# Batch 0 of a spectral layer multiplied in whole float32, and part of batch 1's first DFT placed ahead of the first feed-forward chunk

## The chip, the cores and the metric

The kernel runs on one core of one Trainium2 chip. The metric is the time of one execution in microseconds (us), lower is better. A core has a matmul engine (PE, with its weight loads shown as PEld), a vector engine (DVE), an activation engine (ACT), a general engine (POOL) and a queue (SP) that in this kernel issues all the DMAs. The engines run beside each other, each strictly in the order of its own instructions, and wait for each other through semaphores.

## The reference

```python
X = np.fft.rfft(x, axis=1)                      # x: 8 batches, 3008 times, 256 features
Yr = Xr @ w_r - Xi @ w_i + b_r                  # complex 256x256 linear layer
Yi = Xr @ w_i + Xi @ w_r + b_i
Yr = np.sign(Yr) * np.maximum(np.abs(Yr) - 0.01, 0.0)     # soft threshold, Yi likewise
y = np.fft.irfft(Yr + 1j * Yi, n=3008, axis=1)
h = y.reshape(24064, 256) @ w_in                # w_in, w_out: float64, 2048 wide
out = (h - np.tanh(h)) @ w_out
```

## The kernel before

The transform of length 3008 = 64 x 47 is done in two steps each way, all as matmuls. For each batch:

- **forward** (class `Forward`): 8 loads of `xt` (96 x 4 x 256), each in two parts of 512 columns. A part is multiplied by the constant `f1` (94 x 96) and written as `a` to a scratch tensor in DRAM.
- **spectrum** (class `Spectrum`): 12 units `jp`. Each reads back one `at` tile (128 x 512) of `a`, does the second DFT step with four matmuls (line 277), the linear layer (`cross` and `shared`, line 299), the threshold (`shrink`, line 334 onward), and the first inverse step with the constant `i1` (`inverse`, lines 359 to 361), and writes `z` to DRAM.
- **FFN** (class `Chunk`): 470 columns of time at a time. `time` reads five column groups of `z` as `zin` and does the second inverse step (line 394), `up` multiplies by `w_in` (line 407) and takes h - tanh(h), `down` multiplies by `w_out` (line 428). There are 16 steps `f` to a chunk; chunks 0 and 1 run interleaved as the first 32 steps.

Most products are made with a **split**: an operand is cast on ACT to a float32r part `hi` (line 90), DVE or POOL subtracts it to give `lo` (line 91), and three float32r matmuls (`hi·lo`, `lo·hi`, `hi·hi`) replace one float32 matmul. Two products run in whole float32 already: line 277 and line 394. A whole float32 matmul appears in the trace as two PE records, a float32r one as one.

The float64 weights come as raw words (`w_raw`, 512 KB a piece, 16 pieces) and are rebuilt on the chip. I call that a conversion here: six DVE instructions, three on ACT and two on POOL for each piece (`split_f64`, lines 164 to 180).

The order up to the first FFN step is written out by hand: warm-up matmuls, the whole forward stage of batch 0, the 12 spectrum units of batch 0 with four conversions spread between them, three more conversions, then `time` of chunks 0 and 1. In the loop over `i`, unit `i` is transformed while unit `i-1` is multiplied, unit `i-2` is thresholded and an older one goes through `inverse`. After that a table of slots (`put`, `run`) hangs the remaining conversions, the forward stage of batch 1 (16 parts from slot 8 on) and later batches onto the FFN steps; there the order on each engine is set by a scheduler.

Tiles come from pools with a few buffers for each tag; a tile that takes a buffer waits until its last reader is done. DMAs are issued by SP in program order, so one that waits for a buffer holds back all that are queued behind it.

Of the kernel before, what the change touches and what calls it, by code (L numbers as in the profile page):

```python
# [66 lines left out]
def spectral_ffn(ctx, tc, x, w_r, w_i, b_r, b_i, w_in, w_out, f1, f2, i1, i2, out):  # L67
# [31 lines left out]
    def split_const(ap, shape, name, queue):  # L99
        t = work.tile(shape, F32, name=f"{name}_f", tag="tmp", bufs=4)  # L100
        queue.dma_start(out=t, in_=ap)
        return split(t, name)

    def load_linear():
        wr = load.tile([P, 2, D], F32, name="wr_f", tag="at", bufs=3)
# [8 lines left out]
    def split_linear(wr, wi, bias, zero):  # L114
        w2 = work.tile([P, 2, D], F32, name="w2_f", tag="tmp", bufs=4)
        w3 = work.tile([P, 2, D], F32, name="w3_f", tag="tmp", bufs=4)
# [11 lines left out]
        w3 = split(w3, "w3")  # L128
        w2 = split(w2, "w2", rest=nc.gpsimd)
        w1 = split(wr, "w1", rest=nc.gpsimd)  # L130
        return w1, w2, w3, bias, (ones, brow)
# [67 lines left out]
    class Forward:  # L199
# [15 lines left out]

        def dft(self, q):
# [32 lines left out]
    class Spectrum:  # L249
        def __init__(self, b, jp, first=False):  # L250
            self.b, self.jp, self.first = b, jp, first
            self.rest = nc.gpsimd if first and jp < NJ // 2 - 2 else nc.vector

        def temp(self, name, tag):
            if self.first:
                return ffn.tile([P, 2, D], F32, name=name, tag=tag)
            return work.tile([P, 2, D], F32, name=name, tag="tmp", bufs=4)
# [7 lines left out]
        def dft(self):  # L265
            self.dft0()
            self.dft1()
            self.sums()

        def dft0(self):  # L270
            ps = self.ps = ps_f.tile([P, 512], F32, name="ps_f2", tag="f")
            pv = ps.rearrange("p (t r j m) -> p t j r m", t=2, r=2, j=2)
            for jj in range(2):
                o = m0[2 * self.jp + jj]
                rhs = f2t.rearrange("p (r u c) -> p r u c", r=2, u=2)[:, :, :, o:o + 32]
                for t in range(2):
                    nc.tensor.matmul(pv[:, t, jj], self.at[:, jj, t * P:(t + 1) * P], rhs, start=True, stop=True)  # L277
            self.xh = work.tile([P, 2, 2, P], F32R, name="xh", tag="sp_h", bufs=3)
# [3 lines left out]
            xi = self.xi = work.tile([P, 2, P], F32, name="xi")  # L282
            nc.scalar.copy(out=xi, in_=ps.rearrange("p (t r m) -> p t r m", t=2, r=2)[:, :, 1, :])

        def dft1(self):
            ps, xi = self.ps, self.xi
            flat = "p t r m -> p (t r m)"
            nc.vector.tensor_tensor(out=self.xl.rearrange(flat), in0=ps, in1=self.xh.bitcast(F32).rearrange(flat), op=ALU.subtract)
            pr = ps.rearrange("p (t r m) -> p t r m", t=2, r=2)
            nc.vector.tensor_tensor(out=xi, in0=pr[:, :, 0, :], in1=xi, op=ALU.add)  # L290

        def sums(self):
            self.s = split(self.xi, f"s_{self.b}_{self.jp}", work, "s")

        def product(self, dst, hi, lo, w, more=False, last=True):
            n = 0
            for lhs, rhs in ((lo, w[0]), (hi, w[1]), (hi, w[0])):
                for t in range(2):
                    nc.tensor.matmul(dst, lhs[:, t], rhs[:, t, :], start=n == 0 and not more, stop=n == 5 and last)  # L299
                    n += 1  # L300

        def cross(self, k):
            if k == 0:
                if self.first:
                    self.vv = ps_h.tile([P, 512], F32, name="ps_v", tag="h")
                    ones, brow = lin[4]
                    nc.tensor.matmul(self.vv, ones, brow, start=True, stop=False)
                else:
                    self.vv = ps_f.tile([P, 512], F32, name="ps_v", tag="f")
                self.product(self.vv[:, :D], self.xh[:, :, 1], self.xl[:, :, 1], lin[2], self.first, not self.first)  # L310
            else:
                self.product(self.vv[:, D:], self.xh[:, :, 0], self.xl[:, :, 0], lin[1], self.first)

        def shared(self):
            if self.first:
                t1 = ps_o.tile([P, 512], F32, name="ps_t1", tag=f"o{self.jp % 2}")
            else:
                t1 = ps_f.tile([P, 512], F32, name="ps_t1", tag="f")
            self.product(t1[:, :D], *self.s, lin[0])
            tb = self.tb = self.temp("tb", "th")  # L320
            if self.first:
                nc.scalar.copy(out=tb[:, 0, :], in_=t1[:, :D])
            else:
                nc.vector.tensor_tensor(out=tb, in0=t1[:, :D].unsqueeze(1).to_broadcast([P, 2, D]), in1=lin[3], op=ALU.add)
            if not self.first:
                self.shrink()
                self.halves()

        def shrink(self):
            tb = self.tb  # L330
            y = self.temp("y", "g")
            for jj in range(2):
                for ri in range(2):
                    nc.vector.tensor_tensor(  # L334
                        out=y[ri * 64:(ri + 1) * 64, jj, :],
                        in0=tb[jj * 64:(jj + 1) * 64, 0 if self.first else ri, :],
                        in1=self.vv[jj * 64:(jj + 1) * 64, ri * D:(ri + 1) * D],
                        op=ALU.add,
                    )
            mn = work.tile([P, 2, D], F32, name="mn", tag="tmp", bufs=4)  # L340
            if self.first and self.rest is nc.gpsimd:
                up = self.temp("up", "th")
                nc.scalar.activation(out=up, in_=y, func=AF.Relu, bias=below)
                nc.vector.tensor_scalar(out=mn, in0=y, scalar1=LAM, scalar2=0.0, op0=ALU.add, op1=ALU.min)
                self.rest.tensor_tensor(out=mn, in0=up, in1=mn, op=ALU.add)
            else:
                nc.vector.tensor_scalar_min(out=mn, in0=y, scalar1=-LAM)
                nc.vector.scalar_tensor_tensor(out=mn, in0=y, scalar=LAM, in1=mn, op0=ALU.max, op1=ALU.add)
            self.mn = mn

        def halves(self):
            where = (ffn, "g", None) if self.first else (work, "sp", 3)
            self.z = split(self.mn, f"z_{self.b}_{self.jp}", *where, rest=self.rest)

        def inverse(self):
# [5 lines left out]
            nc.tensor.matmul(pzv, i1h, zh, start=False, stop=True)  # L361
            zo = work.tile([P, 512], F32, name="zo", tag="tmp", bufs=4)
            nc.scalar.copy(out=zo, in_=pz)
            nc.sync.dma_start(out=rows(z_dram[self.b], self.jp), in_=zo)

# [80 lines left out]
    def plan_forward(b, start, each, ahead):  # L446
        for ch in range(NP // XC):
# [5 lines left out]
    def plan_spectrum(b, start, each, ahead, lag, first=False):  # L453
        for jp in range(NJ // 2):
            s = Spectrum(b, jp, first)
# [19 lines left out]
    with tc.manual_schedule(engines={E.PE, E.Activation, E.DVE, E.Pool, E.SP}):  # L475
# [5 lines left out]
        for i in range(11):  # L481
# [3 lines left out]
        f1h, f1l = split_const(f1, [94, 96], "f1", nc.sync)  # L485
        first = [Forward(0, ch) for ch in range(NP // XC)]
        for f in first[:4]:
            f.load()
        lin_in = load_linear()
        f2t = load_const(f2, [P, 384], "f2")  # L490
# [122 lines left out]
```

## Time and profile before

| | us |
|---|---|
| median of 3 runs | 2736.25 (2736.23 to 2739.11) |
| profiled execution, its own time | 2735.33 |
| its span, first to last instruction | 2733.2 |
| PE busy | 2680.9 (98%) |
| DVE busy | 1772.7 (65%) |
| ACT busy | 1393.0 (51%) |
| POOL busy | 80.0 (3%) |

Rows of a timeline give start, duration, engine, line, operation, output<-input, shape, count, and in brackets the idle time before it with what ended that. Rows of a table of stretches give the length, then busy time and count for each engine, the granted PE clock (1.00 is full), the busy share of the DMA engines and GB/s. PE ends are modelled and overlap the next start, so I take the distance of starts where I can.

### The profile page before, as it was taken

What the parts mean: (1) busy time and instruction counts of PE and PEld (TensorE: products, weight loads), DVE (VectorE), ACT (ScalarE), POOL (GpSimd) and SP (SyncE); (2) the same over time, 40 slices, a digit from 0 to 9 for tenths busy, and PEclk for the clock granted to TensorE, in tenths of its full rate; (3) what the DMA queues carried; (4) which work ended last, traced back from release to release, by engine and by line L of the source; (5) the groups of instructions that cost most, each with busy time, mean ns of one, the idle gap of its engine ahead of it and who ended that gap; (6) DMA issues with size and microseconds to landing.
All of it is one profiled execution on the core that took longest, in us unless ns stands there. A gap on an engine that the chain in (4) does not pass through costs nothing.

```text
span 2733.2 us, 37167 instructions
## 1 busy us (share of the span) xinstructions
PE 2680.9 (98%) x14199; PEld 2392.5 (88%) x14199; DVE 1772.7 (65%) x3084; ACT 1393.0 (51%) x2628; POOL 80.0 (3%) x59
## 2 busy tenths in 40 slices
PE   7699999999999999999999999999999999999999
PEld 5578888999989998899988999889998999998989
DVE  6996776666656766576755666656665666655555
ACT  4565455445464545554455444644546444444445
POOL 2540000000000000000000000000000000000000
PEclk7899999999999999999999999999999999999999
DMA  6442114111131112311114111321104111100000
GB/s 191 124 119 85 50 49 126 49 38 44 37 114 47 43 38 74 89 42 49 35 43 116 42 38 38 101 66 45 53 22 123 41 46 40 35 22 22 19 19 17
DMA packets 105026, 163.50 MB, mean 60 GB/s; under 512 B 7472, under 2 KB 70960, under 8 KB 104752
## 3 DMA queue, kind: packets, MB, share of 16 engines
q1 hardware_dynamic: 104848, 161.13, 19.5%
q8 instruction: 112, 1.84, 0.3%
q14 instruction: 66, 0.54, 0.1%
HBM read 86.13 MB, written 74.97 MB: 59 GB/s over the span
## 4 chain that ended last, share of the span: by engine, by line
PE 91%; DVE 4%; ACT 1%; issue 1%; DMA 0%; POOL 0%; SPq 0%; DVEq 0%; ACTq 0%; POOLq 0%
PE o L428 36%; PE h L407 36%; PE ps_v L299 5%; PE ps_i L394 4%; PE ps_f L277 3%; PE ps_t L299 2%; PE ps_f L220 1%; PE ps_f L222 1%; DVE y L334 1%; PE ps_f L221 1%; PE ps_i L360 1%; PE ps_i L361 1%; PE ps_i L359 1%; DVE g L412 1%; DVE gl L416 0%
## 5 line engine op out<-in xcount | busy, mean ns | idle before, releaser
L412 DVE TENSOR_TENSOR g<-h,th 128x470 f32<-128x470 f32 (+1 forms) x832 | 531.7, 639 | 559.0 <-ACT th L410 551.3
L410 ACT ACTIVATE th<-h 128x470 f32<-128x470 f32 (+1 forms) x832 | 463.1, 557 | 771.0 <-PE h L407 769.3
L416 DVE TENSOR_TENSOR gl<-g,gh 128x470 fp32r<-128x470 f32 (+1 forms) x832 | 531.5, 639 | 289.3 <-ACT gh L414 205.5
L414 ACT CAST gh<-g 128x470 fp32r<-128x470 f32 (+1 forms) x832 | 483.0, 581 | 389.4 <-DVE g L412 381.1
L428 PE MATMUL o<-gh,wout_l 128*128 128x470 f32 (+1 forms) x1664 | 632.5, 380 | 0.1
L428 PE MATMUL o<-gl,wout_h 128*128 128x470 f32 (+1 forms) x1664 | 616.6, 371 | 2.2 <-DVE gl L416 2.2
L428 PE MATMUL o<-gh,wout_h 128*128 128x470 f32 (+1 forms) x1664 | 615.8, 370 | 0.0
L407 PE MATMUL h<-yh,win_l 128*128 128x470 f32 (+1 forms) x1664 | 481.9, 370 | 3.0 <-DVE g L412 2.9
L407 PE MATMUL h<-yl,win_h 128*128 128x470 f32 (+1 forms) x1664 | 480.8, 370 | 0.0
L407 PE MATMUL h<-yh,win_h 128*128 128x470 f32 (+1 forms) x1664 | 480.6, 370 | 0.0
L428 PEld LDWEIGHTS o<-gl,wout_h 128*128 128x128 f32 x1664 | 312.8, 188 | 43.9 <-DVE gl L416 5.2
L407 PEld LDWEIGHTS h<-yh,win_l 128*128 128x128 f32 x1664 | 310.4, 188 | 41.8 <-DVE g L412 6.3
L428 PEld LDWEIGHTS o<-gh,wout_l 128*128 128x128 f32 x1664 | 313.1, 188 | 35.3 <-DVE ot L437 1.3
L407 PEld LDWEIGHTS h<-yl,win_h 128*128 128x128 f32 x1664 | 310.9, 188 | 35.7
L407 PEld LDWEIGHTS h<-yh,win_h 128*128 128x128 f32 x1664 | 311.0, 188 | 35.6
L428 PEld LDWEIGHTS o<-gh,wout_h 128*128 128x128 f32 x1664 | 313.6, 188 | 32.2
L334 DVE TENSOR_TENSOR y<-tb,ps_v 64x256 f32<-64x256 f32 x384 | 160.0, 417 | 3.9
L394 PEld LDWEIGHTS ps_i<-i,zin 96*128 96x128 f32 x1024 | 130.2, 197 | 13.3 <-issue 10.4
L394 PE MATMUL ps_i<-i,zin 96*128 96x94 f32 x1024 | 131.9, 278 | 9.7 <-DMA zin<-z 9.7
L91 DVE TENSOR_TENSOR x_l<-xt,x_h 94x512 fp32r<-94x512 f32 x128 | 91.6, 724 | 48.3 <-ACT x_h L90 48.2
L277 PE MATMUL ps_f<-f,at 128*128 128x128 f32 x768 | 104.3, 278 | 11.9 <-DMA at<-a 11.9
L277 PEld LDWEIGHTS ps_f<-f,at 128*128 128x128 f32 x768 | 101.5, 194 | 16.3 <-issue 7.6
(89 smaller groups left out, 2208.2 us busy)
## 6 DMA issues: line engine op xcount, KB each, us to landing
xt<-in_x SPq DMA_DIRECT2D x64, 384.0 KB, 3.6
at<-a SPq DMA_DIRECT2D x96, 256.0 KB, 2.8
z<-zo SPq DMA_DIRECT2D x96, 256.0 KB, 2.0
out<-ot SPq DMA_DIRECT2D x50, 470.0 KB, 2.9
a<-st SPq DMA_DIRECT2D x56, 384.0 KB, 3.1
zin<-z SPq DMA_DIRECT2D x44, 480.0 KB, 4.2
w_raw<-in_moe_w_in SPq DMA_DIRECT2D x8, 512.0 KB, 5.1
w_raw<-in_moe_w_out SPq DMA_DIRECT2D x8, 512.0 KB, 6.9
```

Source lines behind the costliest of these rows:

```text
L91: rest.tensor_tensor(out=lo, in0=src, in1=hi.bitcast(F32), op=ALU.subtract)
L220: nc.tensor.matmul(pv, f1h, xl, start=True, stop=False)
L277: nc.tensor.matmul(pv[:, t, jj], self.at[:, jj, t * P:(t + 1) * P], rhs, start=True, stop=True)
L299: nc.tensor.matmul(dst, lhs[:, t], rhs[:, t, :], start=n == 0 and not more, stop=n == 5 and last)
L334: nc.vector.tensor_tensor(out=y[ri * 64:(ri + 1) * 64, jj, :], in0=tb[jj * 64:(jj + 1) * 64, 0 if self.first else ri, :], in1=self.vv[jj * ...
L394: nc.tensor.matmul(ps[:, k * 94:(k + 1) * 94], self.zt[:, k, t * P:(t + 1) * P], i2t[:, p * 94:(p + 1) * 94], start=True, stop=True,)
L407: nc.tensor.matmul(h[:, :n], lhs[:, t, f * P:(f + 1) * P], rhs[:, t, :n], start=k == 0, stop=k == 5)
L410: nc.scalar.activation(out=th[:, :n], in_=h[:, :n], func=AF.Tanh)
L412: nc.vector.tensor_tensor(out=g[:, :n], in0=h[:, :n], in1=th[:, :n], op=ALU.subtract)
L414: nc.scalar.copy(out=gh[:, :n], in_=g[:, :n])
L416: nc.vector.tensor_tensor(out=gl[:, :n], in0=g[:, :n], in1=gh[:, :n].bitcast(F32), op=ALU.subtract)
L428: nc.tensor.matmul(self.o[t][:, :n], lhs[:, f, t * P:(t + 1) * P], rhs[:, :n], start=f == 0 and k == 0, stop=f == NF - 1 and k == 2,)
```

## The change

Batch 0 loses its splits. `f1`, `i1` and the three weight matrices of the linear layer are kept whole for it, and a new class `WholeSpectrum` multiplies `xt`, `xf` (the spectrum), `sf` (its sum) and `mn` (the thresholded values) as float32 with one matmul instruction in place of three. The splits of those constants are still made, for batches 1 to 7: `f1` and `i1` between the two stages, the three weights inside the spectrum loop.

The order is new as well: 7 warm-up matmuls in place of 11; all eight `xt` loads issued ahead of the other inputs; in each pass of the loop a fixed number of conversion steps; six conversions inside the loop (four before), none behind it, ten in the FFN slots (nine before); the threshold's last sum on DVE (`join`) and no longer on POOL; the raw weights and the table `i2` loaded piece by piece. The first 8 of the 16 parts of batch 1's forward stage (four loads, `following`) stand behind the last spectrum units and ahead of `time`.

```diff
+    def load_whole(ap, shape, name):
+        t = work.tile(shape, F32, name=f"{name}_f", tag="sp_l", bufs=3)
+        nc.sync.dma_start(out=t, in_=ap)
+        return t
...
+        def whole(self, q):
+            self.ps[q] = ps_f.tile([P, 512], F32, name="ps_f1", tag="f")
+            pv = self.ps[q][:96].rearrange("p (a d) -> p a d", d=D)
+            nc.tensor.matmul(pv, f1f, self.xt[:94, 2 * q:2 * q + 2, :], start=True, stop=True)
...
+    class WholeSpectrum(Spectrum):
...
+        def dft(self):
+            self.transform()
+            self.xf = work.tile([P, 2, 2, P], F32, name="xf", tag="sp_h", bufs=3)
+            nc.scalar.copy(out=self.xf.rearrange("p t r m -> p (t r m)"), in_=self.ps)
+
+        def sum(self):
+            pr = self.ps.rearrange("p (t r m) -> p t r m", t=2, r=2)
+            self.sf = work.tile([P, 2, P], F32, name="sf", tag="s_h")
+            nc.vector.tensor_tensor(out=self.sf, in0=pr[:, :, 0, :], in1=self.xf[:, :, 1, :], op=ALU.add)
+
+        def cross(self):
...
+            for k, (dst, lhs) in enumerate((
+                (self.vv[:, :D], self.xf[:, :, 1]), (self.vv[:, D:], self.xf[:, :, 0]), (self.t1[:, :D], self.sf),
+            )):
+                for t in range(2):
+                    nc.tensor.matmul(dst, lhs[:, t], whole_lin[2 - k][:, t, :], start=k == 2 and t == 0, stop=k > 0 and t == 1)
+
+        def common(self):
+            self.tb = work.tile([P, D], F32, name="tb0", tag="xi")
+            nc.scalar.copy(out=self.tb, in_=self.t1[:, :D])
+
+        def shrink(self):
+            y = self.add(lambda jj, ri: self.tb[jj * 64:(jj + 1) * 64, :])
+            up = self.temp("up", "th")
+            nc.scalar.activation(out=up, in_=y, func=AF.Relu, bias=below)
+            mn = self.mn = work.tile([P, 2, D], F32, name="mn", tag="tmp", bufs=4)
+            nc.vector.tensor_scalar(out=mn, in0=y, scalar1=LAM, scalar2=0.0, op0=ALU.add, op1=ALU.min)
+            self.up = up
+
+        def join(self):
+            nc.vector.tensor_tensor(out=self.mn, in0=self.up, in1=self.mn, op=ALU.add)
+
+        def inverse(self):
+            self.pz = ps_f.tile([P, 512], F32, name="ps_i1", tag="f")
+            nc.tensor.matmul(self.pz.rearrange("p (j e) -> p j e", j=2), i1f, self.mn, start=True, stop=True)
...
-        for i in range(11):
+        for i in range(7):
             nc.tensor.matmul(idle, warm[:, :P], warm, start=True, stop=True)
...
+        for i in range(NU + 1):
+            if unit(i - 2):
+                unit(i - 2).common()
+            if unit(i):
+                unit(i).dft()
+            if unit(i - 2):
+                unit(i - 2).shrink()
+            if unit(i):
+                unit(i).sum()
+            if unit(i - 1):
+                unit(i - 1).cross()
+            if unit(i - 2):
+                unit(i - 2).join()
+            if unit(i - 3):
+                unit(i - 3).inverse()
+                unit(i - 3).put(unit(i - 3).pz)
...
+            if 3 <= i < 6:
+                split_lin(i - 3)
+            for op in ops[:(0, 0, 2, 2, 2, 2, 2, 3, 3, 3, 3, 2, 0)[i]]:
+                op()
+                ops.remove(op)
...
+        for q in range(2):
+            following[0].keep(q)
+        for f in following[2:]:
+            f.load()
+        for f in following[1:]:
+            for q in range(2):
+                f.split(q)
+                f.dft(q)
+                f.keep(q)
```

On PE, one pass through the spectrum loop reads so before (`ps_i` is the first inverse step of an older unit, `ps_t` the shared product, `ps_f` the second DFT step, `ps_v` the cross products, which go on for three rows more):

```order
L359 MATMUL ps_i_720<-z_2_l,i_h 128x512
L360 MATMUL ps_i_720<-z_2_h,i_l 128x512
L361 MATMUL ps_i_720<-z_2_h,i_h 128x512
L299 MATMUL ps_t_727<-w_h,s_5_l 128x256 x2
L299 MATMUL ps_t_727<-w_l,s_5_h 128x256 x2
L299 MATMUL ps_t_727<-w_h,s_5_h 128x256 x2
L277 MATMUL ps_f_744<-f_127,at 128x2x64 x4
L307 MATMUL ps_v<-brow,ones 128x512
L299 MATMUL ps_v<-w_h,xl 128x256 x2
L299 MATMUL ps_v<-w_l,xh 128x256 x2
L299 MATMUL ps_v<-w_h,xh 128x256 x2
```

and now, a whole pass:

```order
L271 MATMUL ps_f_480<-f_129,at 128x2x64 x4
L353 MATMUL ps_v<-brow,ones 128x512
L359 MATMUL ps_v<-w_f,xf 128x256 x4
L359 MATMUL ps_t_500<-wr_f,sf 128x256 x2
L378 MATMUL ps_i_508<-mn,i_f 128x512
```

Eighteen float32r matmuls of 256 columns and three of 512 have become six and one in float32; the four of the DFT step and the one with the biases stay.

On ACT, at the end of batch 0's spectrum, before (`zo` is the copy behind the first inverse step, `z_11_h` belongs to the last unit, `x_0_0_h` is the split of part 0 of load 0 of batch 1, `yh` the output of `time`; rows with `w_` are conversions):

```order
L90 CAST z_11_h<-mn 128x512
L363 COPY zo<-ps_i_1144 128x512
L363 COPY zo<-ps_i_1151 128x512
...
L90 CAST x_0_0_h<-xt 94x512
L90 CAST x_0_1_h<-xt 94x512
L179 CAST win_h<-w_f 128x512
L90 CAST x_1_0_h<-xt 94x512
L179 CAST wout_h<-w_f 128x512
L398 CAST yh<-ps_i_1206 128x470
```

and now, from the last `zo` (`st` is the copy of a part's product, ahead of its store as `a`):

```order
L333 COPY zo<-ps_i_803 128x512
L238 COPY st<-ps_f_791 96x512
L238 COPY st<-ps_f_795 96x512
L90 CAST x_1_0_h<-xt 94x512
L238 COPY st<-ps_f_824 96x512
L90 CAST x_1_1_h<-xt 94x512
L238 COPY st<-ps_f_834 96x512
L90 CAST x_2_0_h<-xt 94x512
L238 COPY st<-ps_f_844 96x512
L90 CAST x_2_1_h<-xt 94x512
L238 COPY st<-ps_f_854 96x512
L90 CAST x_3_0_h<-xt 94x512
```

Between the last `zo` and the first `yh` stand now the casts and copies of the parts, taking turns: the cast of a part is queued behind the copy of the part before it. The list goes on with `st`, `x_3_1_h`, two casts of load 4, the last `st` and `yh`.

On SP, the same place before (`zin` are the loads of chunks 0 and 1):

```order
L364 DMA z_343<-zo 128x512 x7
L211 DMA xt<-in_x 96x1024 x2
L384 DMA zin<-z_343 96x5x256 x2
L211 DMA xt<-in_x 96x1024
L143 DMA w_raw<-in_moe_w_in 128x1024 x2
```

and now:

```order
L334 DMA z_231<-zo 128x512 x5
L398 DMA zin<-z_231 96x5x256 x2
L241 DMA a_605<-st 96x4x256
L208 DMA xt<-in_x 96x1024 x2
L241 DMA a_605<-st 96x4x256
L208 DMA xt<-in_x 96x1024
L241 DMA a_605<-st 96x4x256
```

`zin` stands directly behind the last `z` store; the loads of `xt` 2 and 3, which the parts wait for, have moved behind `zin` and a store of `a`.

More of the change, by code (lines that the diff above doesn't have):

```diff
@@ L444, in put, with plan_forward @@
         slots.setdefault(slot, []).append((fn, a))
-    def plan_forward(b, start, each, ahead):
-        for ch in range(NP // XC):
+    def plan_forward(b, start, each, ahead, first=0):
+        for ch in range(first, NP // XC):
             f = Forward(b, ch)
@@ L504, in spectral_ffn @@
-        lin = split_linear(*lin_in, zero)
+                steps[i][0].whole(steps[i][1])
+            if i >= 1:
+                f, q = steps[i - 1]
+                f.keep(q, nc.vector.tensor_copy if i % 2 == 0 else nc.scalar.copy)
+        whole_lin, bias_rows = combine_linear(*lin_in, zero)
+        f1h, f1l = split(f1f, "f1")
         i1h, i1l = split(i1f, "i1")
-        units = [Spectrum(0, jp, True) for jp in range(NJ // 2)]
+        units = [WholeSpectrum(0, jp) for jp in range(NJ // 2)]
@@ L550, in spectral_ffn @@
+        for op in ops:
             op()
```

210 lines of the change are left out of this document (83 added, 127 removed).

## The prediction

> **What bounds the kernel now.** I read the page first, for the busy shares.
>
> ```profile
> span 2733.2 us, 37167 instructions
> PE 2680.9 (98%) x14199; PEld 2392.5 (88%) x14199; DVE 1772.7 (65%) x3084; ACT 1393.0 (51%) x2628; POOL 80.0 (3%) x59
> ```
>
> PE bounds the kernel, and behind the first 240 us nothing changes. So I read the start in tables of stretches, cut where the granted clock changes: the changes lie 3.41 us or a multiple of it apart.
>
> ```profile
> 7.01:10.42 3.41, 2.90 (x12) 1.00 1.06 264
> 20.66:24.07 3.41, 3.40 (x9) 0.50 1.07 370
> 37.73:41.14 3.41, 3.41 (x14) 0.50 0.91 317
> 41.14:44.55 3.41, 3.41 (x26) 0.97 1.09 303
> 133.29:136.70 3.41, 3.41 (x18) 0.50 0.67 193
> 59.63:108.99 49.36, 38.25 (x245) 31.60 (x244) 45.09 (x81) 30.69 (x66) 29.02 (x23) 0.97 0.35 113
> 138.14:200.75 62.61, 57.38 (x245) 44.34 (x244) 59.18 (x96) 42.11 (x79) 27.66 (x17) 0.98 0.37 107
> 200.75:237.57 36.82, 36.82 (x173) 31.91 (x174) 21.95 (x35) 22.06 (x41) 1.28 (x1) 1.00 0.43 129
> ```
>
> The first five rows list PE alone. Matmuls of 128 rows that fill a stretch (37.73) have the full clock after it. Matmuls of 94 rows (20.66, forward stage) or 96 rows (133.29, `time`) fill theirs and stay at half. Once at full, 94 rows kept it (7.01). The last three rows list PE, PEld, DVE, ACT, POOL: the eight spectrum units from 59.63 to 108.99 take 6.17 us each with DVE busy 45.09 of 49.36, and DVE still bounds the FFN up to 200.75 (59.18 of 62.61). PE alone does after that.
>
> **Forward stage.** What stands there now:
>
> ```profile
> 1.91 5.06 PE L482 MATMUL idle<-warm 128*128 128x512 f32 x11 [1.91 <-DVE below L484]
> 5.26 1.14 ACT L90 CAST x_h<-xt 94x512 fp32r<-94x512 f32 x2 [1.40 <-DMA xt<-in_x]
> 19.47 0.58 ACT L236 COPY st<-ps_f 96x512 f32<-96x512 f32 x1 [1.15 <-DMA a<-st]
> 26.36 0.63 PE L222 MATMUL ps_f<-x_h,f_h 94*96 94x512 f32 x1
> 32.66 2.05 PE L277 MATMUL ps_f<-f,at 128*128 128x128 f32 x8 [5.68 <-DMA at<-a]
> ```
>
> The eleven warm-ups take 0.46 us each, the slow rate, and end when the first part comes. Seven end near 4.9, and the first `xt` still lands at 5.26, so the stretch to 7.01 that the warm-ups filled is filled with 94-row matmuls for its second half. By the rows above those don't raise the clock: I take the whole stage as half clock. The price of a whole float32 matmul:
>
> ```profile
> 51.55 2.08 PE L277 MATMUL ps_f<-f,at 128*128 128x128 f32 x8 [5.32 <-DMA at<-a]
> 79.07 1.06 PE L277 MATMUL ps_f<-f,at 128*128 128x128 f32 x8
> 129.62 8.82 PE L394 MATMUL ps_i<-i,zin 96*128 96x94 f32 x40 [9.67 <-DMA zin<-z]
> 138.14 1.13 PE L407 MATMUL h<-yh,win_l 128*128 128x470 f32 x2
> ```
>
> Two records make one matmul: 128 columns cost 0.52 us at half clock and 0.27 at full, 94 columns 0.44 at half. No row has 256 or 512 columns. In proportion to the columns 512 cost 2.08; by the step from 94 to 128 columns (0.08 for 34) only 0.52 + 384 x 0.0024 = 1.4. I take 1.7, between them, half of that at full clock, and half of it again for 256 columns. By the Trainium skill, FP8 and Floating Point Precision, section TensorE Precision Notes, true float32 takes four passes through the array; so the page speaks against the change, which gives up three passes for four, and four passes of the 0.43 us that a 512-column float32r matmul takes here at half clock make an estimate of 1.72.
>
> Sixteen parts from 5.3 at 1.7 end at 32.5; before, the last of 48 matmuls started at 26.36 and took 0.43 (the distance of starts at half clock: 21.89 and 22.31 below), and 5.9 us (copy, store, reload) later the spectrum began at 32.66. Now that is 38.4: **+5.7**. The splits on ACT and DVE that go return nothing here, as PE is then last. Bounds: -0.2 with the price of 1.4 (5.3 + 22.4 + 5.9), +11.8 with 2.08.
>
> **Spectrum of batch 0.** DVE, one unit before, and the first and last step of a conversion that nothing disturbs:
>
> ```profile
> 45.12 1.70 DVE L334 TENSOR_TENSOR y<-tb,ps_v 64x256 f32<-64x256 f32 x4
> ...
> 84.51 1.71 DVE L334 TENSOR_TENSOR y<-tb,ps_v 64x256 f32<-64x256 f32 x4
> 86.32 0.43 DVE L344 TENSOR_SCALAR mn<-y 128x512 f32<-128x512 f32 x1
> 86.78 0.69 DVE L288 TENSOR_TENSOR xl<-ps_f,xh 128x512 fp32r<-128x512 f32 x1
> 87.38 0.41 DVE L290 TENSOR_TENSOR xi<-ps_f,xi 128x256 f32<-128x256 f32 x1
> 87.72 1.16 DVE L178 SCALAR_TENSOR_TENSOR w_f<-w_f,w_s 128x512 f32<-128x512 f32 x1
> ...
> 118.16 0.42 DVE L164 TENSOR_SCALAR w_s<-w_raw 128x512 uint32<-128x512 uint32 x1
> ...
> 120.36 0.42 DVE L164 TENSOR_SCALAR w_s<-w_raw 128x512 uint32<-128x512 uint32 x1
> ```
>
> By distance of starts a unit now needs `y` 1.81, `mn` 0.46, `sf` 0.34 (as `xi`) and `join` 0.60 (as `xl`): 3.21, where it needed 3.54 (`xl`, `xi`, `s_l` for `sf`, `join`). Five steps of a conversion take 2.20, the sixth 0.60: 2.80. What DVE needs beyond that before: eight units at 3.54 and 7.6 for conversion steps are 35.9 of 49.36, so 13.5 us go with 23 POOL instructions, 0.58 each, mostly instructions that stand longer while POOL runs (`w_f` above: 1.16).
>
> Start to first `y`: two DFT steps at half clock 4.2, biases and cross products 5.5 (0.43 + 6 x 0.85), copy 0.5: 10.2, before 12.5. From there the last `mn` needs 12 x 3.21 - 0.7 (two `sf` lie ahead) = 37.8, six conversions 16.8, the weight split 0.6, two parts' subtractions 1.3, 14 POOL instructions 8.1: 64.6. PE needs 1.1 + 0.2 + 2.6 + 0.85 = 4.8 a unit at full clock, below DVE's 5.4, and its 128-row matmuls fill a stretch in the first pass, so I let the clock rise there. ACT has three casts or copies fewer a unit, and the weight splits' casts fit beside. Call J the moment the last unit's values are ready for PE: 38.4 + 10.2 + 64.6 = 113.2. Before it was 118.24 (`z_l` below), so J is 5.0 earlier. Bounds of the 64.6: 56.5 without any POOL wait, 72 with each twice as dear.
>
> **The end of the spectrum and batch 1's eight parts.**
>
> ```profile
> 117.55 0.69 DVE L91 TENSOR_TENSOR z_l<-mn,z_h 128x512 fp32r<-128x512 f32 x1 [0.68 <-ACT z_h L90]
> 121.21 2.83 SPq L211 DMA_DIRECT2D xt<-in_x  x2
> 124.26 0.86 SPq L384 DMA_DIRECT2D zin<-z  x2
> ```
>
> Before: J, store of `z`, `zin` issued at 124.26 behind two `xt` loads, `time` at 129.62, first FFN matmul at 138.14 = J + 19.9. PE lay idle for 9.67 of it. The steps of one part, from the forward stage of batch 0, which has the same ones:
>
> ```profile
> 5.92 1.29 DVE L91 TENSOR_TENSOR x_l<-xt,x_h 94x512 fp32r<-94x512 f32 x2 [1.77 <-ACT x_h L90]
> 6.77 0.60 PE L220 MATMUL ps_f<-x_l,f_h 94*96 94x512 f32 x1
> ...
> 21.89 0.63 PE L221 MATMUL ps_f<-x_h,f_l 94*96 94x512 f32 x1
> 22.31 0.63 PE L222 MATMUL ps_f<-x_h,f_h 94*96 94x512 f32 x1
> 22.98 0.59 ACT L236 COPY st<-ps_f 96x512 f32<-96x512 f32 x1 [0.51 <-PE ps_f L222]
> 23.46 0.62 ACT L90 CAST x_h<-xt 94x512 fp32r<-94x512 f32 x1
> ```
>
> Now six of the eight parts come behind J, and on ACT each cast is queued behind the copy of the part before. So they don't overlap: cast to subtraction 0.66 (5.26, 5.92), to PE 0.85 (6.77), two matmuls 0.43 apart (21.89, 22.31) and the third to its copy 0.86 + 0.67, copy to next cast 0.48: 3.5 us a part. J + 3.5 (matmul 1.7, `zo`, two copies) starts the second load's parts, which end at J + 10.5. The third load's `xt` is queued on SP behind `zin` and a store: 1.7 MB, the bytes that took from 121.21 to 129.62 before, so it lands near J + 12. Four more parts: 3 x 3.5 + 2.8, J + 25.3. `time` as before at half clock, 8.5: J + 33.8. The `zin` wait is hidden, but the chain that hides it is 14 us longer than the wait was. FFN start: 147.0, against 138.14: **+8.9**. Bounds: J + 25 if PE is at full clock throughout (parts 2.8, `time` 4.4), J + 38 if `xt` is 4 us later.
>
> **FFN.** 24 matmuls of 0.22 (half of 0.43) go: 5.3 us of PE. DVE, which bounds up to 200.75, gets a tenth conversion (2.8 + 1.2) and loses seven subtractions of 0.6 there, so it is even; parts that filled PE's holes there return nothing. Bounds 3 and 5.3; I take **-4.3**. Everything later is the same.
>
> Sum: +8.9 - 4.3 = +4.6 on the profiled 2735.33, **2740**. The median of before lies 0.9 above that execution, within what this sum can resolve.
>
> **Rivals.** *The forward stage gets the full clock.* For: 94 rows kept it at 7.01, and the stretches may lie elsewhere in another execution; one that ends before 5.9 is nearly filled by seven warm-ups. Against: 20.66. Three parts at 1.7 and 13 at 0.85 end at 21.4, stores held back to 19.47 make it 24, the spectrum starts near 30: 8.4 earlier, 2732. By the Trainium skill, TensorE: Matmul & The Clock Gate, section Part 1, one busy window of about 3.4 us releases the clock, whatever the rows; by that rule this case would be certain, and the rows at 20.66 and 133.29 disagree.
>
> *The spectrum never gets the full clock* (slower). No row shows whole float32 of 128 rows raising it: the stretch from 51.55 began with 2.08 us of it, and 41.14 rose after float32r. At half clock a pass costs PE 2.1 + 0.4 + 5.1 + 1.7 = 9.3 in place of 5.4 on DVE: eleven times 3.9, less the two inverse steps and the DFT step that the first and last passes lack, 37, so 2777. It decides from a pass over 5.4 us.
>
> *DVE runs free.* `join` leaves POOL, and what is left there may meet other instructions: without waits J is 8 earlier, 2732.
>
> **How the numbers follow.** The forecast has 0.48, its own range 2734 to 2748; full clock in the forward stage 0.22, DVE free 0.18, half clock in the spectrum 0.12. About 0.2% (5.5 us) is what a measurement can tell from no change. Faster: half of each 2732 case and a tenth of the forecast, 0.25. Slower: 0.38 of the forecast and the slow spectrum, 0.30. Same: 0.45. The range 2726 to 2754 leaves out the slow spectrum and the far ends.
>
> **What would show it.** Granted clock 0.50 from 5 to 32 and parts 1.7 apart; spectrum start at 38; first `y` 10 later, `y` groups 5.4 apart at full clock; J near 113; ACT taking turns at 3.5 a part; `time` at J + 25; FFN at 147. A clock of 1.00 at 12 or a spectrum below 5 us a unit makes it wrong to the fast side; 9 us a unit to the slow.

## The result, and the profile after

| | before | after |
|---|---|---|
| median of 5 runs, us | 2736.23 (2735.59 to 2739.11) | 2748.98 (2746.12 to 2756.96) |
| ratio of the times | | 1.0051, 95% interval 1.0032 to 1.0071 |
| profiled execution, its own time | 2735.33 | 2756.96 |
| its span | 2733.2 | 2755.1 |
| PE, DVE, ACT, POOL busy, us | 2680.9, 1772.7, 1393.0, 80.0 | 2709.2, 1739.2, 1374.6, 50.0 |

The changed kernel is half a per cent slower. Its five times stand in two groups, 2746 to 2749 and 2755 to 2757, and the profiled execution belongs to the upper one. The busy times are the first thing to see, in the page's line for the changed kernel (busy us, share of the span, instructions):

```profile
PE 2709.2 (98%) x14095; PEld 2391.7 (87%) x14095; DVE 1739.2 (63%) x3055; ACT 1374.6 (50%) x2575; POOL 50.0 (2%) x39
```

PE has 104 instructions fewer and is busy 28 us longer. It gains 16.5 us of that before chunk 0 ends, and 11.8 spread over all chunks behind.

PE in the forward stage and at the start of the spectrum, from the changed kernel's timeline (start, duration, engine, line, operation, output<-input, shape, count, idle time before):

```profile
5.52 27.59 PE L216 MATMUL ps_f<-xt,f_f 94*96 94x512 f32 x32 [0.25 <-DMA xt<-in_x]
39.16 3.75 PE L271 MATMUL ps_f<-f,at 128*128 128x128 f32 x16 [6.05 <-DMA at<-a]
48.80 1.06 PE L271 MATMUL ps_f<-f,at 128*128 128x128 f32 x8
```

Thirty-two records are sixteen matmuls, 1.72 us each: half clock from end to end. Four matmuls of the second DFT step take 1.9 us of PE at 39.16 and 1.0 at 48.80: in between the clock has risen. The granted clock of the table of stretches reads 1.00 for all of it, because the clock's record of this execution begins only at 48.7 us, with the full clock; before that the durations tell the clock.

```profile
5.50:33.00 27.50, 27.48 (x32) 1.00 0.82 223
```

DVE, first and last unit of the spectrum:

```profile
49.40 1.71 DVE L316 TENSOR_TENSOR y<-tb,ps_v 64x256 f32<-64x256 f32 x4 [5.41 <-ACT tb L363]
110.76 1.71 DVE L316 TENSOR_TENSOR y<-tb,ps_v 64x256 f32<-64x256 f32 x4
113.26 0.69 DVE L374 TENSOR_TENSOR mn<-up,mn 128x512 f32<-128x512 f32 x1 [0.33 <-ACT up L368]
```

J, the end of the last `join`, is 113.95; the units lie 5.6 us apart on average. PE behind J:

```profile
114.10 2.05 PE L378 MATMUL ps_i<-mn,i_f 128*128 128x512 f32 x2 [0.98 <-DVE mn L374]
119.03 0.74 PE L222 MATMUL ps_f<-x_l,f_h 94*96 94x512 f32 x1 [2.88 <-DVE x_l L91]
122.62 0.71 PE L222 MATMUL ps_f<-x_l,f_h 94*96 94x512 f32 x1 [2.00 <-DVE x_l L91]
129.43 0.74 PE L222 MATMUL ps_f<-x_l,f_h 94*96 94x512 f32 x1 [5.24 <-DVE x_l L91]
132.98 0.74 PE L222 MATMUL ps_f<-x_l,f_h 94*96 94x512 f32 x1 [1.96 <-DVE x_l L91]
...
141.43 8.68 PE L408 MATMUL ps_i<-i,zin 96*128 96x94 f32 x40
149.81 1.13 PE L421 MATMUL h<-yh,win_l 128*128 128x470 f32 x2
```

Parts of one load are 3.5 us apart, because of the turns that casts and copies take on ACT; before the third load's first part PE waits 5.24. The `zin` wait is gone, and the FFN starts at 149.81 against 138.14.

Then the chunks. `ot` is the copy of a chunk's output, the last thing done with it. DVE's timeline, the copy of chunk 0 before and after, and two late chunks of each:

```profile
243.63 0.65 DVE L437 COPY ot<-o 128x470 f32<-128x470 f32 x1
...
2512.09 0.65 DVE L437 COPY ot<-o 128x470 f32<-128x470 f32 x1
2554.66 0.65 DVE L437 COPY ot<-o 128x470 f32<-128x470 f32 x1
```

```profile
253.24 0.65 DVE L451 COPY ot<-o 128x470 f32<-128x470 f32 x1
...
2531.75 0.65 DVE L451 COPY ot<-o 128x470 f32<-128x470 f32 x1
2574.59 0.65 DVE L451 COPY ot<-o 128x470 f32<-128x470 f32 x1
```

The changed kernel is 9.61 us behind at chunk 0 and 19.93 behind at 2574.59. Nothing jumps in between: a late chunk takes 42.84 us in place of 42.57, with the same instructions in the same order at full clock, and every chunk adds its share, 11.6 us by the last.

Start distances of the FFN's matmuls, in ns, show how. Three FFN steps of a late chunk, one letter a matmul in PE's order (a, b, c are `up` with `win_l`·`yh`, `win_h`·`yh`, `win_h`·`yl`; x, y, z are `down`), and # where the next one starts more than 212 ns later:

```
before              after
aabbccxyzxyz        aabbccxy####
aabbccxyzxyz        #a##ccxyz##z
aabbccxyzxyz        ##bbccxyzxyz
```

Over 260 us of late chunks (some 1160 distances below 230 ns) the mean is 210.1 ns before and 211.5 after: 30% of them are at 215 in place of 210 (1% before). The pattern repeats after three steps, and three is the number of buffers of `th`, `g`, `gh` and `gl`.

### The profile page after: what moved, and what is told of

Read it like the earlier page. It is cut to its first block, busy times and chain, and to the rows that moved or that the text cites. A ratio compares the mean times of both kernels' runs of the same rounds, so it can differ in the third digit from the quotient of the medians.

```text
span 2755.1 us, 36840 instructions
## 1 busy us (share of the span) xinstructions
PE 2709.2 (98%) x14095; PEld 2391.7 (87%) x14095; DVE 1739.2 (63%) x3055; ACT 1374.6 (50%) x2575; POOL 50.0 (2%) x39
## 4 chain that ended last, share of the span: by engine, by line
PE 91%; DVE 2%; ACT 1%; issue 0%; POOL 0%; ACTq 0%; DVEq 0%; POOLq 0%
PE o L442 37%; PE h L421 37%; PE ps_v L291 4%; PE ps_i L408 4%; PE ps_f L271 3%; PE ps_t L291 2%; PE ps_f L222 1%; PE ps_f L224 1%; PE ps_f L223 1%; PE ps_i L327 1%; PE ps_i L326 1%; PE ps_i L328 1%; DVE gl L430 0%; DVE g L426 0%; DVE y L316 0%
## 5 line engine op out<-in xcount | busy, mean ns | idle before, releaser
L421 PEld LDWEIGHTS h<-yh,win_h 128*128 128x128 f32 x1664 | 312.0, 189 | 39.1
L91 DVE TENSOR_TENSOR x_l<-xt,x_h 94x512 fp32r<-94x512 f32 x112 | 77.2, 696 | 64.2 <-ACT x_h L90 64.0
```

The costliest lines, as they stand in the source:

```text
L91: rest.tensor_tensor(out=lo, in0=src, in1=hi.bitcast(F32), op=ALU.subtract)
L421: nc.tensor.matmul(h[:, :n], lhs[:, t, f * P:(f + 1) * P], rhs[:, t, :n], start=k == 0, stop=k == 5)
```

## The experiments

Theory: the profiled difference has three parts: the forward stage at half clock and a long end of the spectrum, the eight parts of batch 1 on the path, and a slower pace of all chunks that something outside the order sets. The first rival for the pace was the execution itself (another chip, another moment). The first four kernels ran on one chip.

**same_again**: no edit.

> The changed kernel once more, nothing edited. In its first profile the extra 21.2 us came in three pieces: forward stage and end of the spectrum +11.7 at the FFN start, -2.1 in the first FFN chunks, and +11.5 spread evenly over the 50 chunks behind (42.85 us a chunk against 42.57). Theory A (the pace of the chunks belongs to the execution or the chip, not to the change): in this profile a chunk takes 42.57 again or the same as in the other kernels of this call, and the time lies near 2746. Theory B (the change itself slows the chunks): 42.85 again, in this kernel and in every other that keeps the change, and the time lies near 2757. Theory C (the difference between 2746 and 2757 is the clock of the forward stage): the spectrum starts at 39 in a slow one and near 30 in a fast one.

2746.59 (2745.41 to 2754.97; before, on the same chip, 2736.38). Theory A falls: 42.85 again, and in all three kernels below too. Theory C fits the two groups: the profile is of the upper group (2754.97) and its spectrum starts at 39.07; three runs lie at 2745.4 to 2746.6, two at 2754.3 and 2755.0, 8.5 apart. No execution of a lower group was profiled in this kernel; what one looks like is seen in the next kernel, whose forward stage is the same code. Over all kernels with seven warm-ups, the three profiles of an upper execution (the changed kernel, this one, gl512_look0) have all sixteen parts at 1.72 us and a spectrum that starts between 39.1 and 40.9; the four of a lower one (look0, overlap, gl512, conv8) have their first thirteen parts done in under 13 us and a start between 32.0 and 32.8.

**look0**: no part ahead of `time`.

```diff
-        LOOK = 4
+        LOOK = 0
-            if i in (8, 9):
-                following[i - 8].load()
...
-        for f in following[1:]:
-            for q in range(2):
-                f.split(q)
-                f.dft(q)
-                f.keep(q)
```

> None of batch 1's parts ahead of the first time step; all 16 hang on FFN slots, from slot 8 on, as before the change. If the eight parts ahead are what costs (theory): the time step starts about 11 us behind the last unit in place of 27.5, the FFN starts near 134 in place of 149.8, and its first two chunks give back 2 to 5 us, so the kernel is 11 to 14 us faster than the changed one, that is at or a little below the kernel before. Rival (the zin wait and DVE in the first chunks take most of it back): less than 6 us faster.

2736.03, 10.6 less than same_again, a little under the 11 to 14 expected. PE's timeline, forward stage and end of the spectrum:

```profile
5.36 11.99 PE L216 MATMUL ps_f<-xt,f_f 94*96 94x512 f32 x26
19.97 5.17 PE L216 MATMUL ps_f<-xt,f_f 94*96 94x512 f32 x6 [2.62 <-DVE st L238]
32.61 3.75 PE L271 MATMUL ps_f<-f,at 128*128 128x128 f32 x16 [7.47 <-issue]
...
115.12 8.85 PE L408 MATMUL ps_i<-i,zin 96*128 96x94 f32 x40 [6.95 <-DMA zin<-z]
123.67 1.13 PE L421 MATMUL h<-yh,win_l 128*128 128x470 f32 x2
```

Here thirteen parts take 11.99 us, 0.92 each: full clock. Then PE waits 2.62 for a buffer of `st` and is at half clock again, and the spectrum starts at 32.61, where before had 32.66. With J at 106.04 `time` starts at J + 9.1 and the FFN at J + 17.6; with the parts ahead it was J + 27.5 and J + 35.9. The FFN gives back less than that: from its start to the first `ot` copy it took 108.85 us here (to 232.52) and 103.43 with the parts ahead, so eight parts are worth 5.42 there, and 18.2 in front of it.

**overlap**: the same eight parts, each cast ahead of the copy before it, the third load ahead of `zin`.

```diff
+        following[2].load()
         u11.put(u11.pz)
         for c in range(2):
             chunks[c].load()
...
+            f.dft(q)
+            if k + 1 < len(rest):
+                g, r = rest[k + 1]
+                g.split(r)
+                if r == 1 and g is following[1]:
+                    following[3].load()
+            f.keep(q)
```

> The eight parts stay ahead of the time step, but on ACT the cast of a part stands ahead of the copy of the part before it, and the third xt load is issued ahead of the last z store and of zin. If the turn-taking on ACT and the late third load are what makes the chain long (theory): parts 1.5 to 2 us apart in place of 3.5, no wait of 5 us in front of the fifth, the time step 14 to 18 us behind the last unit in place of 27.5, the FFN starts 9 to 13 us earlier, and the time falls by as much. Rival (the chain is bound by the transfers of xt and zin in any order): the time step stays within 4 us of 27.5.

2739.64, 7.0 less than same_again, where 9 to 13 was expected. PE, from the last unit's inverse step on:

```profile
106.90 2.04 PE L378 MATMUL ps_i<-mn,i_f 128*128 128x512 f32 x2 [0.98 <-DVE mn L374]
110.85 0.74 PE L222 MATMUL ps_f<-x_l,f_h 94*96 94x512 f32 x1 [1.91 <-DVE x_l L91]
112.43 0.71 PE L222 MATMUL ps_f<-x_l,f_h 94*96 94x512 f32 x1
114.36 0.74 PE L222 MATMUL ps_f<-x_l,f_h 94*96 94x512 f32 x1 [0.37 <-DVE x_l L91]
115.91 0.74 PE L222 MATMUL ps_f<-x_l,f_h 94*96 94x512 f32 x1
122.50 0.74 PE L222 MATMUL ps_f<-x_l,f_h 94*96 94x512 f32 x1 [4.99 <-DVE x_l L91]
...
125.17 8.68 PE L408 MATMUL ps_i<-i,zin 96*128 96x94 f32 x40
```

Parts are 1.5 to 1.9 apart, the third load no longer waits, and `time` starts at J + 18.4 (J is 106.75). So the turns on ACT and the late third load were the long chain. What stays is the fourth load, which waits 4.99 for its `xt` behind `zin`. Without parts the kernel is still 3.6 us faster (2.8 between the lower groups alone: five of the eleven runs here and four of look0's eleven are in an upper one).

**warm18**: `range(7)` of the warm-ups becomes `range(18)`.

> Eighteen warm-up matmuls in place of seven. Theory (what raises the clock is a full stretch of 128-row matmuls, and 94-row matmuls keep it): the warm-ups run at half clock, 0.43 us each, until a stretch is full, the parts follow 0.86 apart in place of 1.72 and end near 23, the spectrum starts near 30 in place of 39.2, the time falls by 8 to 9 us. Rival 1 (94-row matmuls let the clock fall again): the parts go back to 1.72, the spectrum starts near 42, 3 us slower. Rival 2 (in most executions the forward stage has the full clock anyway): no gain, 1 to 3 us slower.

2746.63 in the median (same_again 2746.59), with all five runs from 2744.8 to 2747.5. The spectrum starts at 31.11. More warm-ups take away the upper group and gain nothing on the lower one: rival 2. In the other two kernels with eighteen (the last two below) no execution lies apart either, fifteen in all; of the 53 runs with seven warm-ups (all but gl480's single one), sixteen do.

**gl512**: the text of the change explains what three buffers have to do with it. A rotation gets buffers as wide as its widest tile. Before, the lo half of batch 0's thresholded values (`z_l`, 512 columns) used the rotation of `gl`; with the splits of batch 0 it went, and `gl` itself has 470 columns. In the built programs the buffers of `th`, `g` and `gh` have the same addresses before and after; those of `yh`, `yl`, `zo` and `ot` moved, and so did two of `gl`:

```
gl buffers, byte in the partition    before 222880, 224928, 226976    after 222880, 224768, 226656
```

```diff
-            gl = ffn.tile([P, CT], F32R, name="gl", tag="g_l")
+            gl = ffn.tile([P, 512], F32R, name="gl", tag="g_l")
```

> The changed kernel with one number edited: the buffers of gl are 512 columns wide again in place of 470 (the change took the last 512-wide tile out of that rotation of three, so that the buffers shrank from 2048 to 1888 bytes and the second and third moved). So far all five kernels that keep the change take 42.85 us for a late chunk, on two chips, against 42.57 before, and in each group of three FFN steps the same 11 of 36 matmuls start 213 to 219 ns apart where the others are at 209 to 211. Theory (the place of the gl buffers sets the pace): a late chunk takes 42.57 again, the slow matmuls are gone, and the time falls by 11 to 12.5 us from the changed kernel's 2746.6. Rival (the longer pitch is from something else, the instruction stream or the moved yh, yl and zin): 42.85 stays and the time does not move.

2735.71 (before, on the same chip, 2735.67): 10.9 less than same_again, just under the 11 to 12.5 expected. DVE's `ot` copies of the same two late chunks:

```profile
2513.93 0.65 DVE L451 COPY ot<-o 128x470 f32<-128x470 f32 x1
2556.50 0.65 DVE L451 COPY ot<-o 128x470 f32<-128x470 f32 x1
```

42.57 again, and the slow matmuls are gone (mean 210.1 ns, 1% above 212). Only `gl` has other addresses here than in the changed kernel, so the moves of `yh`, `yl`, `zo` and `ot` cost nothing that shows.

**gl480**: the same line with 480, a single run (2740.68).

> As the one before with 480 columns, 1920 bytes: the second and third buffer of gl lie at other addresses than in either kernel, but all three at the same remainder to 64 bytes, as with 2048 bytes (with 1888 the second has another). If the remainder to 64 bytes matters: 42.57 a late chunk. If the place at steps of 2048 bytes matters: 42.85 or a number between.

```profile
2516.44 0.65 DVE L451 COPY ot<-o 128x470 f32<-128x470 f32 x1
2559.10 0.65 DVE L451 COPY ot<-o 128x470 f32<-128x470 f32 x1
```

42.66, a third of the loss, with 12% slow matmuls. The remainder to 64 bytes, which is the same for all three buffers here and in gl512, is not what decides; the place at a wider step is.

**before_gl470**: the counter-test, in the kernel before.

```diff
-            self.z = split(self.mn, f"z_{self.b}_{self.jp}", *where, rest=self.rest)
+            if self.first:
+                hi = ffn.tile([P, 2, D], F32R, name=f"{z}_h", tag="g_h")
+                lo = work.tile([P, 2, D], F32R, name=f"{z}_l", tag="sp_l", bufs=3)
...
```

> The kernel before, with one thing changed: the lo half of batch 0's thresholded values goes to another pool, so that the gl buffers are 470 columns (1888 bytes apart), at the same three addresses as in the changed kernel; nothing else of the FFN differs from before. Theory (the place of gl alone sets the pace of the chunks): a late chunk takes 42.85 us in place of 42.57, with the slow matmuls in the same places of a group of three steps, and the kernel is 11 to 12.5 us slower than before, give or take what the other pool costs in the spectrum (0 to 5). Rival (the place matters only with the change's other moves, of yh, yl and ot): 42.57, and 0 to 5 us slower.

2746.96 against 2736.17, ratio 1.0038 (1.0025 to 1.0052): 10.8 slower. In its built program no other buffer of the FFN lies elsewhere than before. Its first `ot` copy is at 244.72, 1.1 behind; then

```profile
2522.92 0.65 DVE L445 COPY ot<-o 128x470 f32<-128x470 f32 x1
2565.77 0.65 DVE L445 COPY ot<-o 128x470 f32<-128x470 f32 x1
```

42.85, with the slow matmuls of the changed kernel in the same places (30% above 212 ns). The place of two `gl` buffers alone sets the pace.

**gl512_look0**: both edits.

> Both edits: 512-wide gl, and none of batch 1's parts ahead of the first time step. If the two costs are independent: 2736.0 less 11 to 12.5, 2723.5 to 2725, some 12 us below the kernel before. Rival (they share a cause): 2730 or more.

2723.05, ratio to before 0.9953 (0.9940 to 0.9967). The two costs add: by the sum of the two savings (10.6 and 10.9) it would be 2725.1, and the 2.1 beyond that stay open. What is left of the change, whole float32 and the new order, is worth 12.6 us to the good.

**fwd_split** (on gl512): the forward stage of batch 0 by splits, eleven warm-ups.

```diff
+        f1h, f1l = split(f1f, "f1")
-                steps[i][0].whole(steps[i][1])
+                steps[i][0].split(steps[i][1])
+            if 1 <= i <= len(steps):
+                steps[i - 1][0].dft(steps[i - 1][1])
```

> The changed kernel with 512-wide gl, and batch 0's forward stage made by splits again, with eleven warm-ups (three float32r matmuls a part); i1 lies in another buffer for it. The kernel with 512-wide gl alone took 2735.7 in the median, with a second group of executions near 2742.5, and its spectrum started at 32.6 in the profile (39.1 in two profiles of the changed kernel). Theory (whole float32 in the forward stage costs nothing where the clock rises in it, and 6.5 to 8 us where it does not): the spectrum starts at 32 to 33.5, the median stays within 1.5 us of 2735.7, and the group near 2742.5 is gone. Rival (the whole matmuls cost 5.7 us in every execution, as the prediction had it): 5 to 6 us faster in the median.

2735.16 (2734.3 to 2737.9, eleven runs), 0.5 below gl512's median and without its two runs at 2741 and 2744; the spectrum starts at 33.28. Its eleven warm-ups are a second difference: warm18 lost the upper group by warm-ups alone, so this run does not show that the splits remove it. In most executions whole float32 costs the forward stage nothing, in the others 6.5 to 8.5 us.

**conv8** (on gl512_look0): two more conversions ahead of `time`.

```diff
+            if i in (8, 9):
+                raws.append(load_f64(1, i - 6, work, "st"))
...
-        for op in ops:
+        for op in ops + convert([(1, k, raws[4 + k]) for k in (2, 3)]):
...
-    for i in range(2):
-        put(2 * i - 2, ffn_weights, 1, 2 + i)
```

> The one before, with two more conversions ahead of the first time step (eight in place of six; they stand behind the last unit, where PE waits for zin) and eight in the FFN slots in place of ten. From the FFN's start to the end of chunk 0 the kernel before took 105.49 us with nine conversions and 16 parts there, the look0 kernel 108.85 with ten and 16. Theory (in these chunks DVE is the bound, and a conversion costs about 2.8 us): that stretch takes 103 to 104, the time step starts at most 1 us later, and the kernel is 3 to 5 us faster than the one before it. Rival (the conversions delay the time step or hide in the FFN anyway): within 1 us.

2720.62, 2.4 less than gl512_look0; the expected 3 to 5 was too much. From the FFN's start (121.98) to the first `ot` copy (228.17) it took 106.19, against 109.41: a conversion in these chunks costs 1.6 us by the two profiles and 1.2 by the medians, not 2.8. The profiles are less alike than the medians: that of gl512_look0 is of its upper run, and the table of stretches has it at half clock once in those chunks, with DVE busy all the time, which conv8's has not:

```profile
174.28:181.11 6.83, 5.95 (x15) 4.92 (x16) 6.83 (x11) 4.31 (x8) 4.36 (x2) 0.50 0.66 190
```

`time` starts at J + 9.0 as without them.

**best** (on conv8): eighteen warm-ups, and four parts where PE waits for `zin`.

```diff
+        for f in following:
+            for q in range(2):
+                f.split(q)
+                f.dft(q)
...
+        for f in following:
+            for q in range(2):
+                f.keep(q)
```

> 512-wide gl, eight conversions ahead of the first time step, eighteen warm-ups, and four of batch 1's 16 parts (two loads, issued inside the spectrum loop) behind the last unit, where PE waits for zin. Theory: the four parts hide in the wait and 12 matmuls of 0.21 us leave the FFN, so 2.5 us below the 2720.6 of the kernel without them, near 2718, and no second group of slower executions. Rival (the parts' casts and copies and the conversions on ACT and DVE delay the time step): 2721 to 2726.

2725.11, a miss: 4.5 slower than without the parts. Timeline of ACT and PE:

```profile
119.47 2.03 ACT L238 COPY st<-ps_f 96x512 f32<-96x512 f32 x4
...
120.10 8.21 PE L408 MATMUL ps_i<-i,zin 96*128 96x94 f32 x37 [8.16 <-ACT st L238]
```

The copies stood behind the conversions on ACT, and `time` needed the PSUM buffers that they empty.

**best2** (on best): copies and stores ahead of the conversions, whose raw words lie in another buffer.

```diff
-                raws.append(load_f64(1, i - 6, work, "st"))
+                raws.append(load_f64(1, i - 6, work, "yl"))
...
             if k + 1 < len(rest):
                 g, r = rest[k + 1]
                 g.split(r)
+            f.keep(q)
```

> As the run named best, but the four parts' copies and stores stand ahead of the two conversions, and the conversions' raw words lie in the yl buffers, so that the copies need not wait for them. In best the time step started 18.4 us behind the last unit's values, after 8.16 us of waiting for the copies of the parts, queued behind the conversions on ACT; in conv8, without parts, it started 9.0 us behind them. Theory (that queue alone ate the gain): the time step starts 10 to 12 us behind the last unit, and the kernel takes 2718 to 2720. Rival (ACT and DVE have no room for parts and conversions before the time step's own casts): the FFN starts later by what the parts add, and the kernel takes 2721 to 2724.

2718.37, ratio to before 0.9936 (0.9922 to 0.9950), the fastest here.

```profile
112.38 0.63 PE L222 MATMUL ps_f<-x_l,f_h 94*96 94x512 f32 x1
115.32 8.85 PE L408 MATMUL ps_i<-i,zin 96*128 96x94 f32 x40 [1.45 <-DMA zin<-z]
```

`time` starts at J + 11.9 (J is 103.38), and best, counted in the same way, had J + 17.7. The four parts hide in the `zin` wait but for some 3 us, and the FFN, from its start to the first `ot` copy, takes 102.25 in place of conv8's 106.19. The same work makes the kernel 4.5 us slower than conv8 or 2.3 faster, by its order on ACT and the buffer of the raw words, which were not tried apart. Of the 2.3, the parts give about 1 between the profiles (3.9 less 2.9); another 1.0 is an earlier J (103.38 against conv8's 104.40), in a kernel that also has more warm-ups.

## Why the prediction was right, and where it was not

The median of 2748.98 lies in the range of 2726 to 2754, but 9 us above the forecast of 2740 and outside the forecast's own 2734 to 2748, and slower had a chance of 0.30 against 0.45 for no change. That it lies in the range is in part luck: in the forecast's own case, half clock in the forward stage, the two executions of the upper group took 2754.88 and 2756.96, above the range, and the median is that of the other case, where an unforeseen loss of 11 us stands against a rival's gain of 8. Step by step, for the profiled execution, which is the forecast's own case:

| step | predicted | profiled |
|---|---|---|
| spectrum start | 38.4 | 39.16 |
| start to first `y` | 10.2 | 10.24 |
| first `y` to J | 64.6 | 64.55 |
| J to `time` | 25.3 | 27.5 |
| FFN start against before | +8.9 | +11.7 |
| FFN, to the end of chunk 0 | -4.3 | -2.1 |
| everything later | 0 | +11.6, and 0.7 behind the last copy |

- **The price of whole float32.** 1.7 us for 512 columns was taken between 1.4 and 2.08; 1.72 was measured, and 0.86 at full clock (by starts: an inverse step of the changed kernel at 57.02, the next matmul at 57.88). The lower bound of that stage was added up wrongly: 5.3 + 22.4 + 5.9 is 33.6, which is 0.9 later than 32.66 and not 0.2 earlier; nothing else rests on it. The spectrum rose to full clock in its first pass, so the slow rival is out.
- **Spectrum.** The sum held to 0.1 us, by luck in one term. The 8.1 us for "14 POOL instructions" stood for DVE instructions that take longer while POOL runs. Fourteen POOL instructions did run there, but only one DVE instruction was drawn out by more than 0.1 us (a `w_f`, 1.76 in place of 0.69). In their place DVE waited for ACT, a term that the prediction put at nothing (the casts "fit beside"). The changed kernel's waits of DVE from 50.00 to 113.95, us in total, times, longest:

```profile
DVE y L316 <- ACT tb L363: 4.7, 6, 1.0
DVE w_l L91 <- ACT w_h L90: 1.5, 1, 1.5
DVE mn L374 <- ACT up L368: 0.7, 2, 0.3
DVE x_l L91 <- ACT x_h L90: 0.3, 1, 0.3
```

  That is 7.2 us. ACT's copy `tb` stood each of the six times behind a cast of a conversion that had itself waited for a step of DVE. So "DVE runs free" did not happen, but not because of POOL.
- **J to `time`.** The mechanism was right: turns of 3.5 us on ACT, the `zin` wait hidden by a longer chain; overlap and look0 confirm it. The size was 2.2 short in this execution and 0.5 in same_again's (25.8): the third load's first matmul came at J + 15.5 here, not at about J + 13.5.
- **FFN.** The eight parts are worth 5.4, as the prediction's 5.3 had it. The step that was wrong is that DVE "is even" with a tenth conversion: conv8 puts 1.2 to 1.6 on a conversion. look0, with before's number of parts and one conversion more, takes 3.4 longer than before there; 1.2 to 1.6 is the conversion, some 0.5 the pace of the two chunks in it, and the other 1.3 to 1.7 were not settled.
- **"Everything later is the same."** This step failed, and it is half of the profiled loss. The deleted `halves` kept three buffers 2048 bytes apart. The prediction followed the order of instructions and their durations, and left out where tiles lie. gl512 and before_gl470 show the cause from both sides, 10.9 and 10.8 us.
- **The clock of the forward stage.** The rival that had 0.22 is what most executions do: by their times, 3 of the 5 runs here. Its 8.4 us agree with the 8.5 between the groups, but not step by step: it had the spectrum start near 30, and the profiles of lower groups have 32.0 to 32.8, because the last three parts fell back to half clock (look0, 19.97: 5.17 us for three). By that case the prediction said 2732; without the `gl` loss the kernel takes 2735.7, and the misses of the FFN and of `time`, up to 2.2 each, are of the size of the rest.

For the clock, the Trainium skill, TensorE: Matmul & The Clock Gate, section Part 1, says that one busy window of about 3.4 us brings the full clock; "whatever the rows" is the prediction's reading of it. The profiled execution disagrees: 27.48 of 27.50 us busy with 94-row matmuls, eight times that length, at 1.72 us each. In the profiled executions with seven warm-ups and full clock the rise is on record between 5.8 and 7.6 us, behind a stretch that the warm-ups share with the first parts; afterwards 94-row matmuls keep it until PE waits for 2.6 us (19.97 in look0). A wait of 0.27 at the same place in warm18 left it: its last three parts took 2.81 us, 0.94 each.

## What to carry to other kernels

A deleted tile can move the tiles that stay: a pool's buffer is as wide as its widest user, so when a change removes a user, compare the addresses of the inner loop's buffers before and after, and measure the pace of a late, untouched iteration first; a difference there is not in the edited code. Work put into a wait is free only if all its engines are free in that wait: look at the queue of the engine that copies and casts (3.5 us a part by turns, 1.5 to 1.9 in the other order), and at what is queued behind a load. When an execution can take either of two clocks at its start, work out both and expect two groups of times.

## What was not expected of the hardware

Matmuls of identical shape, order and clock started 215 ns apart in place of 210 for three in ten of the FFN's, through the place of two 1880-byte buffers: 160 and 320 bytes lower (after) cost 0.28 us a chunk, 128 and 256 bytes lower (gl480) 0.09. Most of the slow matmuls do not read `gl`: of the eleven in the pattern above two are z, five are `up` matmuls. Which access meets which was not tried. The Trainium skill, SBUF — State Buffer, section SBUF: two separate sides, says that on the engine side only the port pair that DVE and GpSimd share leads to waiting, and that PE never waits for another engine there; these runs show a matmul pitch that depends on an operand buffer's place, while no GpSimd instruction runs (none behind 253 us). The measurement decides that the place matters; whether PE waits for another engine or reads more slowly stays open.
